# Reordering the start of a two-stage attention and MLP kernel: two weight blocks and the next batch's x change places in the load queue

## The chip, the cores and the metric

The kernel runs on one core of a Trainium2 chip. The metric is device time in microseconds (us) of one execution; less is better. A core has five engines that run side by side, each with its own in-order queue: TensorE (PE, matrix products, results to the small memory PSUM), VectorE (DVE), ScalarE (ACT), GpSimd (POOL) and SyncE (SP). They wait for each other by semaphores. Data moves between main memory and the on-chip SBUF by DMA.

## The reference

Two stages. In the first, for each of 8 batches and 8 heads, x (512 rows of 64) and a state (32 rows of 64) read each other; in the second, all 8 x 544 = 4352 rows of 512 go through a two-layer network with an exact gelu.

```python
scores = scale * x @ state.T          # scale = 1/8; softmax over 32
xread  = softmax(scores) @ state      # 512 x 64 per head
scores2 = scale * state @ x.T         # softmax over 512
sread  = softmax(scores2) @ x         # 32 x 64 per head
rows = concat([xread, sread], rows).to(4352, 512)
out  = gelu(rows @ w_in) @ w_out      # 512 -> 2048 -> 512
```

All inputs and the output are float32; the kernel computes in bfloat16 and sums in float32.

## The kernel before, in words

**The work.** The xread of a batch is never formed. Instead `pmat`/`p_mm` multiply the batch's state with `w_in` (a product P, in four column chunks f of 512; `p_copy` takes the two halves from PSUM to SBUF, one on ScalarE and one on VectorE), and `mm1(b, m)` multiplies P's block m of 128 columns with the transposed softmax weights AT and applies gelu on ScalarE to give block m (of 16) of g. `M(k)` is `mm1` of block k counted over all batches, so M(4) to M(7) are blocks 4 to 7 of batch 0 and M(16), M(17) blocks 0 and 1 of batch 1. The second layer of batch 0 is done by `mm2_m(0, m)`: block m of g times block m of `w_out`, four matmuls that add into four PSUM tiles. (From batch 1 on, the second layer is done by a scheme with seven products of quarter size, `X`, whose sums of weights `w_sums` and sums of g `g_sum` are made on VectorE.)

**The attention part of batch 1.** `begin(1)`; `xtr(1, ...)` transposes x on TensorE, 32 matmuls in two PSUM tiles, copied by VectorE to `xT`; `scores` multiplies it with the state and applies Exp on ScalarE to give `e`; `norm(1, half)` sums, inverts and scales `e` to `a` on VectorE; `atr(1)` transposes `a` into `AT`. `rearr_ones(1)` copies x into the layout `xo` that the state's reading needs, on VectorE for batches 0 and 1. `sread(b)` is that reading, 32 small matmuls of `e` with `xo` into the PSUM tile `sr`; `sread_out(b)` divides by the sums on VectorE to give `srm`; `srt(b)` transposes that and VectorE copies it to `XSR`, which the last batch's slot uses (`read_out_slot`, b = 7).

**The order.** It is written by hand: the calls from line 969 on are issued in the order they stand, and each engine runs its own instructions of them in that order. Nothing is rescheduled. Loads of weights, of x from batch 1 on and of the state (all but batch 0's) are issued from POOL's queue and land in the order of issue: first `w_in` columns 0 to 511, `w_out` blocks 0, 1, batch 1's state, blocks 2, 3, `w_in` 512 to 1023, then `load_x(1)`, and then `load_rest()`: blocks 4, 5, blocks 6, 7, `w_in` 1024 to 1535, blocks 8 to 11, `w_in` 1536 to 2047, batch 2's state, batch 2's x, blocks 12 to 15, batch 3's x. An issue waits for the landing of the one eight places before it, whose semaphore it takes over.

**PSUM.** There are eight banks. Four (`ps_f`, `ftile`) are a ring for short-lived tiles: `xT_ps`, `sr`, `pt`, `srT`, `p_ps`, `hp`, `aT_ps` of batch 1. The n-th tile waits until the (n-4)-th has been copied out. The other four (`ps_o`, `otile`) hold the four sums `op` of batch 0 until `mm2_m`/`U` end at group 15. `burst([...])` issues two products (four `ftile`s), then their four copies.

**ScalarE's tables.** Exp and Gelu need different tables; a switch is one ACT_TABLE_LOAD, 1.28 us. `exp_table()` forces a switch to Exp early by a one-element activation on `spare`.

**`warm`** is an SBUF tile of zeros for the dummy matmuls `keep_warm` before the first weights are there; it is not used after them.

The lines that the change moves stand at 126 to 143 (loads), 991 to 1067 (order), 1096 to 1114 and 1116 to 1132 (batch 2 and the loop over batches, eight slots p per batch). The functions follow.

Of the kernel before, what the change touches and what calls it, by code (L numbers as in the profile page):

```python
# [9 lines left out]
FP32 = mybir.dt.float32  # L10
BF16 = mybir.dt.bfloat16
AF = mybir.ActivationFunctionType
ALU = mybir.AluOpType
# [4 lines left out]
def kernel(  # L18
# [8 lines left out]
    nc = tc.nc  # L27
# [49 lines left out]
    sb0 = persist.tile([128, 2, 2, 2, NS], BF16, name="sb0")  # L77
    hold = persist.tile([128, 1], BF16, name="hold")
    spare = persist.tile([128, 1], FP32, name="spare")
    warm = persist.tile([128, 512], BF16, name="warm")  # L80
    xos = [persist.tile([128, SJ, HC, 132], BF16, name=f"xo_{i}") for i in range(2)]
    x4s = [persist.tile([128, SJ, HC, 128], BF16, name=f"x4_{i}") for i in range(2)]

# [28 lines left out]
    def load_w_out(m0, m1):  # L112
        nc.gpsimd.dma_start(out=w_out_bf[:, m0:m1, :], in_=w_out_r[:, m0:m1, :])  # L113

    def load_x(b):
        xb = xin.tile([128, H, SJ * D], BF16, name="xb", tag="xb")
        nc.gpsimd.dma_start(out=xb, in_=xr[b])
        xbs[b] = xb
# [13 lines left out]


    def load_rest():
        load_w_out(4, 6)
        load_w_out(6, 8)
        load_w_in(1024, 1536)
        load_w_out(8, 12)
        load_w_in(1536, 2048)
        load_st(2, 3)  # L140
        load_x(2)
        load_w_out(12, 16)
        load_x(3)
# [178 lines left out]
    def exp_table():  # L322
        nc.scalar.activation(out=spare, in_=spare, func=AF.Exp)
# [23 lines left out]
    def norm(b, half):  # L347
        A = atts[b]
        G = SJ * 2
        hs = slice(64 * half, 64 * half + 64)  # L350
        e4 = A.e[:, :, hs].rearrange("p g (c n) -> p g c n", n=NS)
        cs = att.tile([128, G, 2], FP32, name="cs", tag="cs")
        nc.vector.reduce_sum(out=cs, in_=e4, axis=AX.X)  # L353
        ics = att.tile([128, G, 2], FP32, name="ics", tag="ics")
        nc.vector.reciprocal(out=ics, in_=cs)
        nc.vector.tensor_tensor(  # L356
            out=A.a[:, :, hs].rearrange("p g (c n) -> p g c n", n=NS),
            in0=e4,
            in1=ics[:, :, :].to_broadcast((128, G, 2, NS)),
            op=ALU.mult,  # L360
        )
# [24 lines left out]
    def sread(b):  # L386
        A = atts[b]
        A.sr = ftile([128, 2, 65], "sr")
        for t in range(2):
            for j in range(SJ):  # L390
                for c in range(HC):
                    nc.tensor.matmul(  # L392
                        A.sr[32 * c:32 * c + 32, t, :],
                        lhsT=A.e[:, 2 * j + t, 32 * c:32 * c + 32],
                        rhs=A.xo[:, j, c, 1 + 65 * t:66 + 65 * t],
                        start=(j == 0),
                        stop=(j == SJ - 1),
                    )

    def sread_out(b):  # L400
        A = atts[b]
        A.srm = att.tile([128, 2, D], BF16, name="srm", tag="srm")
        flat = A.sr.rearrange("q t d -> q (t d)")
        inv = att.tile([128, 2], FP32, name="inv", tag="inv")
        nc.vector.reciprocal(out=inv, in_=flat[:, 0:130:129])
        nc.vector.tensor_tensor(
            out=A.srm,
            in0=flat[:, 1:129].rearrange("q (t d) -> q t d", t=2),
            in1=inv[:, :].to_broadcast((128, 2, D)),
            op=ALU.mult,  # L410
        )
# [31 lines left out]
    def pmat(b, f):  # L443
        p_copy(b, f, p_mm(b, f, ftile))
# [4 lines left out]
    def burst(chunks, b_read=None):  # L449
        done = []  # L450
        first = len(chunks) < 4 and b_read is not None
        if first:
            sread(b_read)
        for i, (b, f) in enumerate(chunks):
            done.append((b, f, p_mm(b, f, ftile if i < 2 else otile)))
        for x in done[:2]:
            p_copy(*x)
        if b_read is not None and not first:
            sread(b_read)
        for x in done[2:3]:  # L460
            p_copy(*x)
        if b_read is not None:
            sread_out(b_read)
        for x in done[3:]:
            p_copy(*x)
# [66 lines left out]
    def mm2_m(b, m):  # L532
        for j in range(SJ):
            if m == 0:
                ops[b, j] = otile([128, d_model], "op")
            nc.tensor.matmul(  # L536
                ops[b, j],
                lhsT=gs[b][:, m, j * 128:(j + 1) * 128],
                rhs=w_out_bf[:, m, :],
                start=(m == 0),  # L540
                stop=(m == MC - 1),
            )
# [16 lines left out]
    def w_sums(i):  # L559
        (b11, b12), (b21, b22) = w_q  # L560
        w_add(*(
            ("3", b12, b22, ALU.subtract),
            ("4", b21, b11, ALU.subtract),
            ("6", b11, b12, ALU.add),
            ("1", b11, b22, ALU.add),
            ("7", b21, b22, ALU.add),
        )[i])
# [347 lines left out]
    def M(*ms):  # L915
        for m in ms:
            mm1(m // MC, m % MC)
# [70 lines left out]
    keep_warm(6)  # L988
    sums0(1)
    norm0(0)  # L990
    load_x(1)
    scores0(3)
    sums0(2)
    sums0(3)
# [36 lines left out]
    burst([(1, 0), (0, 1)])  # L1031
    mm2_m(0, 3)
    M(4, 5)
    M(6)
    begin(1)
    xtr(1, (0, 1))
    xtr(1, (2, 3))
    sread(0)
    sread_out(0)
    M(7)  # L1040
    scores(1, 0)
    scores(1, 1)
    srt(0)
    mm2_m(0, 4)
    mm2_m(0, 5)
    rearr_ones(1)
    mm2_m(0, 6)
    norm(1, 0)
    sread(1)
    pmat(0, 2)  # L1050
    sread_out(1)
    norm(1, 1)
    mm2_m(0, 7)
    M(8, 9)
    M(10, 11)
    mm2_m(0, 8)
    atr(1)
    mm2_m(0, 9)
    w_sums(2)
    burst([(1, 1), (0, 3)])  # L1060
    mm2_m(0, 10)
    M(16, 17)
    M(12, 13)
    srt(1)
    M(14, 15)
    mm2_m(0, 11)
    w_sums(0)
# [30 lines left out]
    def home(shape, name):  # L1098
        at = next(homes)
        return ftile(shape, name) if at is None else otile(shape, name, at)  # L1100

    p0 = p_mm(2, 0, home)
    p1 = p_mm(2, 1, home)
    nc.scalar.copy(out=Ps[2][:, 1, 512:1024], in_=p1[1])
# [11 lines left out]
    for b in range(2, B):  # L1116
        nb = b + 1
        for p in range(8):
            k = 16 * b + 2 * p
            if p == 1 and nb < B:  # L1120
                scores(nb, 0)
                scores(nb, 1)
            if p in (2, 3) and nb < B:
                norm(nb, p - 2)
            if p == 3 and nb + 1 < B:
                xtr_dma(nb + 1)
            if p == 5 and nb < B:
                atr_dma(nb)
            if p == 7 and nb < B:
                srt(b)  # L1130
                if nb == B - 1:
                    srt(nb)
            if nb == B and p < 5:
                read_out_slot(p)
                if p == 4:
                    r_homes()
                    r_sum("5")
                    r_sum("2")
                continue
            M(k, k + 1)  # L1140
            if b == 2 and p in (0, 3):
                pmat(2, 2 + p // 3)
            if b == 2 and p == 1:
                w_sums(4)
            if p < 5:
                if p == 0:
                    g_sum(b - 1, "5")
                    if b > 2:
                        sr_w("5216"[b - 3])
                X(b - 1, "45127"[p])  # L1150
                if p < 3:
                    g_sum(b - 1, "127"[p])
            if p == 0 and b + 3 < B:
                hold_for(b, 0)
                load_x(4 if b == 2 else b + 3)
            if p == 6 and b == 2:
                hold_for(b, 12)
                load_x(5)
            if p == 0 and nb + 1 < B:
                begin(nb + 1)  # L1160
                rearr(nb + 1)
            if nb == B:
                if p == 5:
                    g_sum(b, "6")
                    R("3")
                    r_sum("1")
                    R("4")
                    r_sum("6")
                    r_sum("7")
                if p == 6:  # L1170
                    R("5")
                    X(b, "3")
                    R("2")
                    R("1")
                if p == 7:
                    R("6")
                    X(b, "6")
                continue
            if p == 5:
                g_sum(b, "6")  # L1180
                reads = (b, nb) if nb == B - 1 else (b,)
                for r in reads:
                    sread(r)
                p_run(nb, (0, 1), ((0, 1), (3, 2)))
                for r in reads:
                    sread_out(r)
                if b == 2:
                    rearr_ones(3)
                elif nb + 1 < B:
                    rearr_ones(nb + 1)  # L1190
            if p == 6:
                X(b, "3")
            if p == 7:
                if b == 2:
                    rearr_ones(4)
                p_run(nb, (2, 3), ((1, 2), None))
                X(b, "6")
# [41 lines left out]
```

## Time and profile before

| what | value |
|---|---|
| median of 3 runs | 203.81 us (203.44 to 204.97) |
| profiled execution, first to last instruction (its span) | 202.5 us |
| TensorE busy, share of the span | 196.6 us, 97% |
| VectorE / ScalarE / POOL busy | 157.1 (78%) / 135.4 (67%) / 67.9 us (34%) |
| TensorE clock granted | 1.00 throughout |
| DMA, 16.6 to 36 us | 187 to 207 GB/s |
| DMA, 52 to 202 us | 91 GB/s |

The profile gives for the profiled execution no other time than its span; the runs' times cover what lies around it as well. In its lines a row is one instruction or several merged ones: start in us from the span's beginning, duration in us (ns in group lists), the engine (PEld is TensorE's weight load), the line of the code, the operation, output tile <- input tiles, sizes, how many, and in brackets how long the engine stood idle before it and what ended that. A matmul's end is modelled, and matmuls overlap, so the distance between two starts tells the pace, not the duration.

### The profile page before, as it was taken

To read this page: it belongs to the slowest core of one execution; us is meant where nothing else is said; L and a number is where in the kernel's file an instruction comes from. 1 tells how busy PE (TensorE), PEld (TensorE's weight loads), DVE (VectorE), ACT (ScalarE), POOL (GpSimd) and SP (SyncE) were. 2 spreads that over 40 slices of the span, in tenths; PEclk is the share of its full clock that TensorE was granted. 3 is DMA by queue.
4 is the path that set the end of the run, shared out by engine and by line. 5 is a ranking of instruction groups with operands and counts; after the bars stand their busy time and mean duration, and the time that the engine had idled before them with its cause. 6 is when DMAs were issued, how large, how long until landed. Compare 5 with 4: busy or idle time off the path is not lost.

```text
span 202.5 us, 4900 instructions
## 1 busy us (share of the span) xinstructions
PE 196.6 (97%) x2035; PEld 132.6 (65%) x2035; DVE 157.1 (78%) x255; ACT 135.4 (67%) x240; POOL 67.9 (34%) x75
## 2 busy tenths in 40 slices
PE   7898999999999999999999999999999999999994
PEld 2433544465667577766776687567775787878893
DVE  2953776789998979878897787768778988895882
ACT  3785577699885779566967596687847576864120
POOL 8962603323249555360627502430220002200000
PEclk9999999999999999999999999999999999999999
DMA  6999999977675788782774308440107001040125
GB/s 203 174 174 203 205 199 197 181 134 142 96 135 107 207 104 108 155 179 32 90 163 142 77 0 123 130 119 0 52 9 202 3 0 55 0 159 0 52 102 162
DMA packets 40566, 23.16 MB, mean 114 GB/s; under 512 B 21856, under 2 KB 39136, under 8 KB 40544
## 3 DMA queue, kind: packets, MB, share of 16 engines
q0 software_dynamic: 13984, 8.10, 29.3%
q1 hardware_dynamic: 25872, 14.36, 28.5%
q10 hardware_dynamic: 688, 0.39, 0.6%
q8 instruction: 16, 0.26, 0.5%
q14 instruction: 6, 0.05, 0.1%
HBM read 17.30 MB, written 8.91 MB: 129 GB/s over the span
## 4 chain that ended last, share of the span: by engine, by line
PE 89%; DMA 5%; POOL 4%; DVE 0%; issue 0%; POOLq 0%
PE xp L591 41%; PE hp L494 26%; DMA xb<-in_x_dram 5%; PE p_ps L429 4%; PE op L536 4%; PE sp L798 3%; PE rp L864 3%; POOL w_in_bf L105 2%; PE op L520 2%; PE xp L703 2%; PE pt L333 2%; PE sr L392 1%; POOL sbd L95 1%; POOL w_out_bf L113 1%; PE xT_ps L271 1%; POOL st_bf L121 0%
## 5 line engine op out<-in xcount | busy, mean ns | idle before, releaser
L501 ACT ACTIVATE g<-hp 128x512 bf16<-128x512 f32 x124 | 67.1, 605 | 27.9 <-PE hp L494 21.3
L494 PE MATMUL hp<-AT,P 128*128 128x512 bf16 x248 | 62.9, 379 | 0.0
L591 PEld LDWEIGHTS <-gsum 128*128 128x128 bf16 x528 | 51.0, 98 | 12.1 <-issue 1.9
L585 DVE TENSOR_TENSOR gsum<-g 128x2048 bf16<-128x2048 bf16 x35 | 45.5, 1314 | 0.1
L591 PE MATMUL xp<-ws,gsum 128*128 128x256 bf16 x304 | 36.3, 273 | 0.0
L494 PEld LDWEIGHTS <-P 128*128 128x128 bf16 x248 | 22.8, 98 | 20.5 <-issue 2.7
L591 PE MATMUL xp<-ws,g 128*128 128x256 bf16 x224 | 26.8, 273 | 0.0
L591 PE MATMUL xp<-w_out_bf,gsum 128*128 128x256 bf16 x224 | 26.6, 273 | 0.0
L591 PEld LDWEIGHTS <-g 128*128 128x128 bf16 x224 | 21.7, 98 | 4.6 <-issue 0.2
L646 POOL TENSOR_TENSOR u<-s,oh 128x512 f32<-128x512 f32 x6 | 8.8, 1466 | 41.1 <-ACT oh L643 41.1
L441 DVE CAST P<-p_ps 128x512 bf16<-128x512 f32 x29 | 18.7, 683 | 3.1 <-PE p_ps L429 2.9
L440 ACT CAST P<-p_ps 128x512 bf16<-128x512 f32 x29 | 15.8, 599 | 5.4 <-PE p_ps L429 5.1
L225 POOL COPY x<-xb 128x1024 bf16<-128x1024 bf16 x12 | 12.6, 1080 | 15.7 <-DMA xb<-in_x_dram 15.7
L235 POOL COPY xo<-xb 128x1024 bf16<-128x1024 bf16 x12 | 14.5, 1234 | 4.6 <-PE sr L392 4.6
L610 POOL TENSOR_TENSOR v<-q,oh 128x512 f32<-128x512 f32 x6 | 8.6, 1434 | 20.6 <-ACT oh L648 20.5
L536 PE MATMUL op<-w_out_bf,g 128*128 128x512 bf16 x48 | 11.8, 380 | 0.0
L356 DVE TENSOR_TENSOR a<-e,ics 128x512 bf16<-128x512 bf16 x14 | 10.7, 764 | 0.5
L429 PE MATMUL p_ps<-w_in_bf,sbd 64*32 64x512 bf16 x248 | 10.5, 382 | 0.0
L353 DVE TENSOR_REDUCE cs<-e 128x16 f32<-128x512 bf16 x14 | 9.5, 677 | 0.7 <-ACT e L340 0.7
L419 DVE COPY XSR<-srT 128x128 bf16<-128x128 bf16 x8 | 5.7, 759 | 5.5 <-PE srT L416 5.5
L501 ACT ACT_TABLE_LOAD x7 | 9.0, 1283 | 0.1
L618 DVE TENSOR_TENSOR oh<-xp,v 128x512 f32<-128x512 f32 x6 | 4.1, 690 | 5.2 <-POOL v L610 5.2
(132 smaller groups left out, 230.2 us busy)
## 6 DMA issues: line engine op xcount, KB each, us to landing
out_dram<-oh SPq DMA_DIRECT2D x15, 256.0 KB, 2.9
xb<-in_x_dram POOLq DMA_DIRECT2D x7, 512.0 KB, 5.9
out_dram<-oh SPq DMA_DIRECT2D x6, 512.0 KB, 2.9
w_in_bf<-in_moe_w_in_dram POOLq DMA_DIRECT2D x6, 256.0 KB, 12.4
out_dram<-osb SPq DMA_DIRECT2D x5, 256.0 KB, 3.2
w_out_bf<-in_moe_w_out_dram POOLq DMA_DIRECT2D x4, 256.0 KB, 8.9
w_out_bf<-in_moe_w_out_dram POOLq DMA_DIRECT2D x2, 512.0 KB, 13.3
x0f<-in_x_dram SPq DMA_DIRECT2D x3, 256.0 KB, 3.7
```

The lines of the kernel that those rows point to most:

```text
L225: nc.gpsimd.tensor_copy(out=A.x4[:, :, :, 64 * t:64 * t + 64].rearrange("p j c d -> p c j d"), in_=src[:, t],)
L235: eng.tensor_copy(out=A.xo[:, :, :, 2 + 64 * t:66 + 64 * t].rearrange("p j c d -> p c j d"), in_=src[:, t],)
L353: nc.vector.reduce_sum(out=cs, in_=e4, axis=AX.X)
L356: nc.vector.tensor_tensor(out=A.a[:, :, hs].rearrange("p g (c n) -> p g c n", n=NS), in0=e4, in1=ics[:, :, :].to_broadcast((128, G, 2, NS) ...
L429: nc.tensor.matmul(ps[t][32 * c:32 * c + 32, :], lhsT=sbd[64 * t:64 * t + 64, b, c, 32 * t:32 * t + 32], rhs=w_in_bf[64 * t:64 * t + 64, c ...
L440: nc.scalar.copy(out=dst[:, 0, :], in_=ps[0])
L441: nc.vector.tensor_copy(out=dst[:, 1, :], in_=ps[1])
L494: nc.tensor.matmul(hp, lhsT=Ps[b][:, t, m * 128:(m + 1) * 128], rhs=atts[b].AT[:, :, t, :], start=(t == 0), stop=(t == 1),)
L501: nc.scalar.activation(out=gs[b][:, m, :], in_=hp, func=AF.Gelu)
L536: nc.tensor.matmul(ops[b, j], lhsT=gs[b][:, m, j * 128:(j + 1) * 128], rhs=w_out_bf[:, m, :], start=(m == 0), stop=(m == MC - 1),)
L585: nc.vector.tensor_tensor(out=t, in0=g_q(b, h0, k0), in1=g_q(b, h1, k1), op=op)
L591: nc.tensor.matmul(ps[:, j - js[0], :], lhsT=lhs[:, m, 128 * j:128 * j + 128], rhs=rhs[:, m, :], start=(first and j == js[0] and m == 0), ...
```

## The change

Batch 1's x and `w_out` blocks 4, 5 change places in POOL's queue. On TensorE, M(7) and the groups `mm2_m(0, 4)` and `mm2_m(0, 5)` are issued ahead of `xtr(1, ...)`, with an explicit `exp_table()` on ScalarE behind M(7)'s gelu. Groups 6 and 7 follow at the places where M(7) and groups 4, 5 stood, so that `pmat(0, 2)` is next to M(8). `norm(1, 1)` moves behind M(8) to M(11), M(16, 17) ahead of the burst, `w_sums(2)` behind the burst. The state reading of batch 1 moves: `sread(1)` down to the products of batch 2, with a ScalarE copy of its result into the memory of `warm`, and its division and transposing to slots 6 and 7 of batch 3.

```diff
     def load_rest():
-        load_w_out(4, 6)
+        load_x(1)
         load_w_out(6, 8)
...
+    def read_raw(b):
+        sread(b)
+        raw = persist.tile([128, 130], FP32, name="sraw", tag="warm")
+        nc.scalar.copy(out=raw, in_=atts[b].sr.rearrange("q t d -> q (t d)"))
+        return raw
+
+    def read_norm(b, raw):
+        A = atts[b]
+        A.srm = att.tile([128, 2, D], BF16, name="srm", tag="srm")
+        inv = att.tile([128, 2], FP32, name="inv", tag="inv")
+        nc.vector.reciprocal(out=inv, in_=raw[:, 0:130:129])
+        nc.vector.tensor_tensor(
+            out=A.srm,
+            in0=raw[:, 1:129].rearrange("q (t d) -> q t d", t=2),
+            in1=inv[:, :].to_broadcast((128, 2, D)),
+            op=ALU.mult,
+        )
...
     norm0(0)
-    load_x(1)
+    load_w_out(4, 6)
     scores0(3)
...
     M(4, 5)
-    M(6)
+    M(6, 7)
+    exp_table()
+    mm2_m(0, 4)
+    mm2_m(0, 5)
     begin(1)
     xtr(1, (0, 1))
     xtr(1, (2, 3))
     sread(0)
     sread_out(0)
-    M(7)
+    mm2_m(0, 6)
     scores(1, 0)
     scores(1, 1)
     srt(0)
-    mm2_m(0, 4)
-    mm2_m(0, 5)
+    mm2_m(0, 7)
     rearr_ones(1)
-    mm2_m(0, 6)
+    pmat(0, 2)
     norm(1, 0)
-    sread(1)
-    pmat(0, 2)
-    sread_out(1)
-    norm(1, 1)
-    mm2_m(0, 7)
     M(8, 9)
     M(10, 11)
+    norm(1, 1)
     mm2_m(0, 8)
     atr(1)
     mm2_m(0, 9)
+    M(16, 17)
+    burst([(1, 1), (0, 3)])
     w_sums(2)
-    burst([(1, 1), (0, 3)])
     mm2_m(0, 10)
-    M(16, 17)
     M(12, 13)
-    srt(1)
     M(14, 15)
...
+    raw1 = read_raw(1)
     p0 = p_mm(2, 0, home)
...
+            if b == 3 and p == 6:
+                read_norm(1, raw1)
             if p == 7 and nb < B:
                 srt(b)
+                if b == 3:
+                    srt(1)
```

More of the change, by code (lines that the diff above doesn't have):

```diff
@@ L79 @@
     spare = persist.tile([128, 1], FP32, name="spare")
-    warm = persist.tile([128, 512], BF16, name="warm")
+    warm = persist.tile([128, 512], BF16, name="warm", tag="warm")
     xos = [persist.tile([128, SJ, HC, 132], BF16, name=f"xo_{i}") for i in range(2)]
```

## The prediction

> **What bounds the kernel now.** I read three views in this order: the chain that ended last, to see which engine sets the end; TensorE's timeline from 17 to 31 us, where all the edits but two lie; and the timelines of ScalarE and VectorE over the same stretch, because an order on TensorE is only as good as the copies that feed it. First the chain's shares from the page, then its one long foreign piece from the chain in order of time:
>
> ```profile
> PE 89%; DMA 5%; POOL 4%; DVE 0%; issue 0%; POOLq 0%
> ```
>
> ```profile
> 8.93 10.95 DMA xb<-in_x_dram
> 19.87 0.04 issue
> 19.92 1.08 PE xT_ps L271 x32
> ```
>
> From 19.9 us on the chain is TensorE and nothing else, up to the last output's add. So every wait of TensorE after 17 us counts in full, work moved about on it counts nothing, and the only prize here is the idle time ahead of batch 1's transposes. TensorE's timeline gives its size (start, us, then in brackets the idle time before):
>
> ```profile
> 17.59 1.50 PE L494 MATMUL hp<-AT,P 128*128 128x512 bf16 x6
> 19.92 1.08 PE L271 MATMUL xT_ps<-ident,xb 128*64 128x128 bf16 x32 [0.82 <-DMA xb<-in_x_dram]
> 20.93 0.43 PE L392 MATMUL sr<-xo,e 128*32 128x65 bf16 x32
> 21.29 0.61 PE L494 MATMUL hp<-AT,P 128*128 128x512 bf16 x2
> 22.41 2.75 PE L536 MATMUL op<-w_out_bf,g 128*128 128x512 bf16 x12
> 25.46 0.41 PE L429 MATMUL p_ps<-w_in_bf,sbd 64*32 64x512 bf16 x8
> 25.80 1.04 PE L536 MATMUL op<-w_out_bf,g 128*128 128x512 bf16 x4
> 26.67 1.89 PE L494 MATMUL hp<-AT,P 128*128 128x512 bf16 x8
> 28.48 1.04 PE L536 MATMUL op<-w_out_bf,g 128*128 128x512 bf16 x4
> 29.35 0.61 PE L374 MATMUL aT_ps<-ident,a 128*128 128x128 bf16 x8
> ```
>
> Starts, not durations, give the pace: eight 512-column matmuls start 26.67 to 28.48, four `op` matmuls 25.80 to 26.67, so 0.216 us each; one lasts 0.38, so a group ends about 0.17 after its last start slot. Then ScalarE and VectorE:
>
> ```profile
> 18.27 1.57 ACT L501 ACTIVATE g<-hp 128x512 bf16<-128x512 f32 x3 [0.73 <-PE hp L494]
> 25.93 0.58 ACT L440 CAST P<-p_ps 128x512 bf16<-128x512 f32 x1 [1.00 <-PE p_ps L429]
> 26.53 1.28 ACT L501 ACT_TABLE_LOAD   x1
> 27.83 2.06 ACT L501 ACTIVATE g<-hp 128x512 bf16<-128x512 f32 x4
> ```
>
> ```profile
> 22.61 0.73 DVE L419 COPY XSR<-srT 128x128 bf16<-128x128 bf16 x1 [0.32 <-PE srT L416]
> 22.97 1.16 DVE L235 COPY xo<-xb 128x1024 bf16<-128x1024 bf16 x2
> 26.09 0.68 DVE L441 CAST P<-p_ps 128x512 bf16<-128x512 f32 x1
> 27.10 0.68 DVE L353 TENSOR_REDUCE cs<-e 128x16 f32<-128x512 bf16 x1
> 28.09 0.69 DVE L356 TENSOR_TENSOR a<-e,ics 128x512 bf16<-128x512 bf16 x1
> ```
>
> What to see: `pmat(0,2)` starts at 25.46 and M(8), which reads its copy, at 26.67, 1.21 later; `mm2_m(0,7)` fills that gap exactly. And `norm(1,1)` ends at 28.78, only 0.57 ahead of the transposes of `a` at 29.35. Both covers are thin, and the change takes both away.
>
> **The change part by part.** I follow TensorE through the new order with these durations.
>
> *The loads.* `w_out` blocks 4, 5 and batch 1's x swap places on POOL's queue. By the DMA view x was issued at 8.93 and landed at 19.87; blocks 4, 5 (9.81 plus 11.3) at 21.1; blocks 6, 7 at 22.4, each pair of blocks 1.3 after the one before; the last `w_in` piece ahead of them (8.32 plus 8.0) landed at 16.3. The queue lands in order, so blocks 4, 5 come at 16.3 + 1.3 = 17.6 and x takes their old place, 21.1. Everything behind them keeps its time. POOL's issue of x moves from 8.93 to about 9.6 behind one more 0.7 us issue, long before its data's turn. x took 3.5 us of the queue; the next batch's equal transfer took 2.7 (behind blocks of the same kind), so 20.3 to 21.7 bounds its landing. I take 21.1, the sum of the bytes ahead of it.
>
> *M(7) and groups 4, 5 ahead of the transposes.* M(4) to M(6) leave the issue slot at 19.92 - 0.82 - 0.17 = 18.93. M(7) adds 0.43, to 19.36; its `hp` buffer is the fourth `p_ps` of the burst, copied by 17.8. Groups 4 and 5 are 8 x 0.216 = 1.73, to 21.09; gelu 4 ended at 18.9 and gelu 5 at 19.4, so they don't wait. x at 21.1 plus an issue delay of 0.1: transposes at 21.2 in place of 19.92, 1.28 later with 0.44 + 1.73 = 2.17 us less left to do. **Gain 0.89**, 0.95 with x at 20.3, 0.35 with x at 21.7.
>
> *Reading 0, group 6, scores, group 7.* From 21.2: transposes 1.01 to 22.2, `sread(0)` 0.36 to 22.6 (blocks 6, 7 in by 22.4), group 6 0.87, scores 0.62, `srt(0)` 0.06, group 7 0.87 with 0.1 at a change of tile shape: `pmat(0,2)` starts at 25.05. Its `w_in` pieces land at 23.7 and 24.9. `exp_table()` puts the Exp load behind gelu 7, 20.3 to 21.7, ahead of the scores; the number of table loads is the same, and its dummy activation is 0.2 us of idle ScalarE. Nothing here costs TensorE.
>
> *`pmat(0,2)` straight before M(8).* The cover, group 7, now runs before it. M(8) still can't start until 1.21 after the first product matmul (the copy on ScalarE ends 1.05 after it), and the matmuls themselves take 0.34: **loss 0.87**, M(8) at 26.26. VectorE's half of the copy follows `rearr_ones` and lands at about the same time, so the bounds are 0.8 and 1.1. Behind M(8) the Gelu load (1.3 from start to start) puts gelu 8 at 27.42 to 28.03, group 8 at 28.1: 1.88 after M(8) where it was 1.81, **0.07**.
>
> The Trainium skill ("ScalarE: Activation LUTs", What ACT_TABLE_LOAD costs) puts a drain of about 1.38 us on top of the 1.28 us load for each switch of set. The rows above show the first gelu 1.30 after the load's start, so with no such drain; by the page, as an estimate, group 8 would start 1.4 later and the total would be 206.7.
>
> *`norm(1,1)` behind M(8) to M(11).* On VectorE the transposed reading of batch 0, `rearr_ones`, the copy of P, `norm(1,0)` and `norm(1,1)` are now one queue: 0.36 + 1.16 + 0.61 + 1.61 + 1.68 = 5.42 us by the starts above, from 24.3 (0.25 after `srt(0)` at 24.05). It ends at 29.7. TensorE is through with group 8 at 28.97 and `atr(1)` needs both halves: it starts at 29.75, **loss 0.75** (0.5 to 0.9). Taking `sread_out(1)` off this queue (0.4 us) is in the sum.
>
> *M(16, 17) ahead of the burst.* `ps_f` is a ring of four. After `atr(1)`'s two tiles come hp16, hp17, and the burst's four: the first product takes the two transposes' buffers, the second product those of hp16 and hp17, which stay full until gelu 16 and 17 are done. M(17) ends its slots at t = 0.86 after M(16)'s start; the first product would be issued by 1.2; gelu 16 runs from 0.62 to 1.22, gelu 17 from 1.11 to 1.71, and its release is seen at 1.78. Loss 1.78 - 1.18 = **0.60** (0.5 to 0.7). Before, the two tiles were long empty.
>
> *The later reading of batch 1.* `sread(1)` (0.36) and `srt(1)` (0.06) move down TensorE's queue and cost it the same. `read_raw`'s copy is one more ScalarE instruction of about 0.5 us ahead of a P copy near 48 us, where ScalarE runs without a gap from 41.8 to 50; TensorE has three groups queued there. Bounds 0 and 0.5; I take 0, since the copy it delays is read two groups later. `read_norm` is 0.45 us on VectorE, hidden by 22% idle. The second `srt` in the group at b = 3 makes two buffers of the ring wait for VectorE: where before has such a pair, at 155.5 us, the product behind it took 0.88 us in place of 0.56, so 0 to 0.32; I take 0.15.
>
> **Sum**: -0.89 + 0.87 + 0.07 + 0.75 + 0.60 + 0.15 = +1.55 us on a span of 202.5. The median of the runs shown, 203.81, is 1.3 above that span; what lies outside the span is not touched. 203.81 + 1.55 = 205.4, and as two of the losses were rounded up, I write 205.3. About 1% (2 us) is what a measurement of this kernel can tell from no change.
>
> **Rivals.**
> *Only the wait goes.* If the three covers hold after all, because copies end sooner than their rows or work slides into the gaps, the time is 203.81 - 0.89 = 202.9. For it: VectorE is 78% and ScalarE 67% busy. Against it: each of the three waits is one consumer straight behind its producer on the same in-order queue. Chance 0.12. It decides if the sum of the new waits is under 0.89; two of the three would have to be gone.
> *x comes late.* If x takes its place behind blocks 4, 5 and still needs more than its 3.5 us, or POOL's ring lets it in late, TensorE waits at the transposes in place of before, 0.1 for each 0.1 past 21.1, and all later waits stay: with x at 21.7 to 22.2, 205.9 to 206.4. Against it: the bytes ahead of x are known. It passes +1% from x at 21.6. Chance 0.23.
> *The edits don't act as described.* The built order shows the moved loads and groups where the diff puts them, so I give this nothing of its own.
>
> **Numbers.** The forecast, net +1.5 with own range 204.5 to 205.9, has 0.62; 0.03 is left for something faster still: in the windows by stage TensorE is busy for 2.50 of the 3.30 us from 16.6 to 19.9 and throughout from 19.9 to 52, so there is no 2 us to be had here. Range 202.9 to 206.5: the low end is the rival without losses, the high end x at 22.2. Faster by over 1%: 0.03. Slower by over 1%: most of the late-x case and the forecast's upper edge, 0.26. Within 1%: 0.71.
>
> **What would show it.** In the changed profile: transposes of x start at 21.0 to 21.3 with under 0.2 us idle before them; M(8) waits 0.8 to 1.0 on the P copy; `aT_ps` waits 0.5 to 0.9 on VectorE's `a`; `p_ps` of the burst waits about 0.6 on gelu; and TensorE has no other wait over 0.2 us up to 60 us. A transposes' start before 20.5, or no wait on M(8), would make the prediction wrong.

## The result and the profile after

| | median | runs | profiled execution: time, span |
|---|---|---|---|
| before | 203.62 us (203.31 to 204.97) | 6 | span 202.5 |
| changed | 206.03 us (205.55 to 206.60) | 6 | 206.49, span 204.7 |

The changed kernel takes 1.0108 times as long, with a 95% interval of 1.0083 to 1.0132: 2.2 us more. In the profiled executions with both a time and a span, the time is 1.77 us over the span (206.49 and 204.72 here, 203.54 and 201.77 in the second profile of before). So, as an estimate from these two, the execution that the prediction was worked out on, with its span of 202.49, took about 204.25 us, more than the median that the sum was then added to. That matters below.

TensorE's timeline of the changed kernel first (start, us, engine, line, operation, tiles, count, in brackets the idle time before it and what ended it):

```profile
17.86 1.89 PE L512 MATMUL hp<-AT,P 128*128 128x512 bf16 x8
19.59 1.89 PE L554 MATMUL op<-w_out_bf,g 128*128 128x512 bf16 x8
21.41 1.08 PE L271 MATMUL xT_ps<-ident,xb 128*64 128x128 bf16 x32
25.14 0.41 PE L447 MATMUL p_ps<-w_in_bf,sbd 64*32 64x512 bf16 x8
26.25 1.90 PE L512 MATMUL hp<-AT,P 128*128 128x512 bf16 x8 [0.70 <-ACT P L458]
28.16 1.04 PE L554 MATMUL op<-w_out_bf,g 128*128 128x512 bf16 x4
29.61 0.62 PE L374 MATMUL aT_ps<-ident,a 128*128 128x128 bf16 x8 [0.41 <-DVE a L356]
31.88 1.22 PE L447 MATMUL p_ps<-w_in_bf,sbd 64*32 64x512 bf16 x16
...
93.28 0.96 PE L447 MATMUL p_ps<-w_in_bf,sbd 64*32 64x512 bf16 x16
```

The wait for x is gone: groups 4 and 5 (19.59) run into the transposes (21.41). Two waits have brackets, 0.70 ahead of M(8) at 26.25 and 0.41 ahead of `aT_ps` at 29.61. Two more can only be read from a row's length, because the wait lies inside a merged row: sixteen product matmuls last 1.22 at 31.88 and 0.96 at 93.28, where the same sixteen take 0.62 or 0.63 when nothing holds them. The engines that TensorE waits for, ScalarE and VectorE:

```profile
25.61 0.59 ACT L458 CAST P<-p_ps 128x512 bf16<-128x512 f32 x1 [0.43 <-PE p_ps L447]
26.21 1.28 ACT L519 ACT_TABLE_LOAD   x1
27.51 2.06 ACT L519 ACTIVATE g<-hp 128x512 bf16<-128x512 f32 x4
31.56 1.09 ACT L519 ACTIVATE g<-hp 128x512 bf16<-128x512 f32 x2 [1.99 <-PE hp L512]
```

```profile
24.74 0.96 DVE L235 COPY xo<-xb 128x1024 bf16<-128x1024 bf16 x2
25.65 0.69 DVE L459 CAST P<-p_ps 128x512 bf16<-128x512 f32 x1
28.86 0.69 DVE L356 TENSOR_TENSOR a<-e,ics 128x512 bf16<-128x512 bf16 x1
```

ScalarE's half of P is done at 26.20 and M(8)'s first matmul, which reads it, follows at 26.25; VectorE's half is done at 26.34, ahead of the second matmul, which starts at 26.48. `a` ends at 29.55 and `aT_ps` follows at 29.61. Each is one consumer straight behind its producer. Inside the burst, the two tiles of the second product start at 32.21 and 32.70, each 0.05 after the end of a gelu, of block 16 (32.16) and of block 17 (32.65, the end of the last ScalarE row).

The kernel before was profiled a second time, in an execution of 203.54 us (span 201.8). It is the better yardstick, because in it x lands at 19.07 and not at 19.87:

```profile
19.12 1.08 PE L271 MATMUL xT_ps<-ident,xb 128*64 128x128 bf16 x32
25.87 1.89 PE L494 MATMUL hp<-AT,P 128*128 128x512 bf16 x8
28.55 0.61 PE L374 MATMUL aT_ps<-ident,a 128*128 128x128 bf16 x8
29.95 0.63 PE L429 MATMUL p_ps<-w_in_bf,sbd 64*32 64x512 bf16 x16
```

No bracket stands at 19.12: **in this execution of the kernel before there is no wait for x, the very thing that the change takes away.** (Its transposes start 0.05 after x lands, so x is only just in time.) From there on every start lies 0.80 to 0.82 earlier than in the first profile, to the end.

The end of the span moved too. SyncE's issues of the last outputs (start, us, queue, line, operation, tensors, count), from the timeline of the kernel before in its second profile, and then of the changed one:

```profile
197.30 1.86 SPq L662 DMA_DIRECT2D out_dram<-oh  x3
```

```profile
199.62 2.09 SPq L680 DMA_DIRECT2D out_dram<-oh  x3
```

The row of the same three issues, from the first's start to the last's end, is 2.09 long in place of 1.86, and in the DMA view of the last 6 us the last output of 64 KB on this queue needs 2.3 us from issue to landing in place of 1.9. From the start of the last add on VectorE to the last landing is 2.09 us in this profile of before and 2.74 in the changed kernel. Between these two profiles the last landing moved by 2.97 us: the last add comes 2.32 later, by TensorE, and the way out takes 0.65 longer.

### The profile page after: what moved, and what is told of

It is laid out like the page before. It is cut to its first block, busy times and chain, and to the rows that moved or that the text cites. A ratio compares the mean times of both kernels' runs of the same rounds, so it can differ in the third digit from the quotient of the medians.

```text
span 204.7 us, 4897 instructions
## 1 busy us (share of the span) xinstructions
PE 197.2 (96%) x2030; PEld 133.1 (65%) x2035; DVE 157.0 (77%) x255; ACT 135.8 (66%) x242; POOL 67.3 (33%) x75
## 4 chain that ended last, share of the span: by engine, by line
PE 90%; DVE 5%; DMA 2%; ACT 1%; issue 1%
PE xp L609 40%; PE hp L512 25%; PE p_ps L447 5%; PE op L554 4%; PE sp L816 3%; PE rp L882 3%; PE xp L721 2%; PE op L538 2%; DMA st_f<-in_state_dram 2%; PE pt L333 2%; PE sr L392 1%; PE hp L1027 1%; PE aT_ps L374 1%; DVE a L356 1%; DVE cs L353 1%
## 5 line engine op out<-in xcount | busy, mean ns | idle before, releaser
L512 PEld LDWEIGHTS <-P 128*128 128x128 bf16 x248 | 23.0, 98 | 21.2 <-issue 2.5
L609 PEld LDWEIGHTS <-g 128*128 128x128 bf16 x224 | 21.7, 98 | 4.6 <-issue 0.2
L447 PE MATMUL p_ps<-w_in_bf,sbd 64*32 64x512 bf16 x248 | 11.5, 383 | 0.1
L340 ACT ACTIVATE e<-pt 128x512 bf16<-128x512 f32 x14 | 7.6, 593 | 2.1 <-PE pt L333 2.0
```

The lines of the kernel that those rows point to most:

```text
L447: nc.tensor.matmul(ps[t][32 * c:32 * c + 32, :], lhsT=sbd[64 * t:64 * t + 64, b, c, 32 * t:32 * t + 32], rhs=w_in_bf[64 * t:64 * t + 64, c ...
L512: nc.tensor.matmul(hp, lhsT=Ps[b][:, t, m * 128:(m + 1) * 128], rhs=atts[b].AT[:, :, t, :], start=(t == 0), stop=(t == 1),)
L609: nc.tensor.matmul(ps[:, j - js[0], :], lhsT=lhs[:, m, 128 * j:128 * j + 128], rhs=rhs[:, m, :], start=(first and j == js[0] and m == 0), ...
```

## The experiments

Theory: the four new waits are additive and cost what their rows say, and the gain is the wait for x. Rivals: the waits are limited by something else than named (the layout copy `rearr_ones`, one P half), or the gain isn't there. Starts of chosen tiles in the profiled executions, in us; the last column is the time from the start of the last add to the last landing:

| kernel | x lands | transposes of x | M(8) | `aT_ps` | M(18) | M(48) | M(64) | last add | tail |
|---|---|---|---|---|---|---|---|---|---|
| before, first | 19.87 | 19.92 | 26.67 | 29.35 | 35.74 | 73.09 | 94.43 | 199.56 | 1.99 |
| before, second | 19.07 | 19.12 | 25.87 | 28.55 | 34.93 | 72.28 | 93.61 | 198.75 | 2.09 |
| changed | 20.21 | 21.41 | 26.25 | 29.61 | 36.50 | 74.20 | 95.93 | 201.07 | 2.74 |
| e1 | 20.17 | 21.21 | 26.05 | 29.40 | 36.30 | 74.00 | 95.72 | 200.85 | 2.65 |
| e2 | 21.46 | 21.50 | 26.34 | 29.70 | 36.00 | 73.72 | 95.44 | 200.58 | 2.71 |
| e3 | 20.81 | 21.23 | 26.08 | 29.43 | 36.33 | 74.03 | 95.36 | 200.55 | 2.72 |
| e4 | 21.93 | 21.97 | 27.20 | 30.49 | 37.38 | 75.08 | 96.81 | 201.95 | 2.93 |
| e5 | 20.02 | 20.07 | 26.82 | 29.50 | 35.88 | 73.23 | 94.56 | 199.70 | 1.99 |
| e6 | 19.90 | 20.93 | 26.45 | 29.59 | 35.97 | 73.31 | 94.65 | 199.78 | 2.00 |
| e7 | 20.64 | 20.79 | 25.77 | 29.02 | 35.32 | 73.03 | 94.37 | 199.55 | 1.99 |
| e9 | 19.14 | 19.18 | 25.93 | 28.62 | 35.00 | 72.34 | 93.68 | 198.82 | 2.13 |
| e10 | 19.66 | 21.28 | 25.71 | 30.88 | 34.78 | 72.48 | 93.82 | 199.01 | 2.73 |
| e11 | 19.84 | 21.26 | 26.95 | 30.71 | 37.66 | 75.00 | 96.34 | 201.48 | 2.39 |
| e12 | 19.79 | 19.83 | 26.23 | 29.13 | 35.42 | 73.12 | 94.85 | 199.99 | 2.93 |

Each ratio below is against runs of the kernel before on the same chip in the same sitting; their medians went from 203.69 to 204.36, so ratios are compared and not microseconds. (e1 to e4 ran on one chip, e5 to e8 on a second, e9 to e12 on a third; the second profile of before is e8.)

**One edit of the changed kernel undone at a time (e1 to e4).**

e1: the layout copy moved behind what was thought to wait for it.

```diff
-    rearr_ones(1)
     pmat(0, 2)
...
     atr(1)
+    rearr_ones(1)
```

> The changed kernel with rearr_ones(1) (two VectorE copies, 0.9 us) moved from ahead of the P copy to behind atr(1); only the state's reading at 47 us needs it now. Theory of the four waits: VectorE reaches norm(1,1) 0.9 us sooner, so the 0.41 us wait of the transposes of a goes; M(8) still waits for ScalarE's half of the P copy (ends 26.2), so that wait stays at 0.6 to 0.7; the kernel is 0.4 to 0.6 us faster than the changed one, 205.5. Rival, that the cost comes from the load order and not from VectorE: no change, 206.0. Rival, that VectorE's half of the P copy and not ScalarE's holds M(8): both waits go and it is 1.1 us faster, 204.9.

Measured: 206.34 us, ratio 1.0083 [1.0051, 1.0116]. The expectation for `aT_ps` failed:

```profile
29.40 0.62 PE L374 MATMUL aT_ps<-ident,a 128*128 128x128 bf16 x8 [0.41 <-DVE a L356]
```

The wait is the same 0.41. With the copy gone VectorE stands idle for 0.54 us ahead of its half of P, because P's product isn't there earlier; what leads up to `a` is product, P's copy (0.61 from start to start), `norm(1,0)` and `norm(1,1)` (1.6 each), all behind the product at 25. So the layout copy only filled time; `norm` is late because it stands behind the P copy. M(8)'s wait stayed at 0.70, by ScalarE's half.

e2: the burst ahead of M(16) and M(17) again.

```diff
-    M(16, 17)
     burst([(1, 1), (0, 3)])
     w_sums(2)
     mm2_m(0, 10)
+    M(16, 17)
```

> The changed kernel with M(16, 17) put back behind the burst and group 10. Theory: the two PSUM tiles of the second product are then those of hp10, hp11, long empty, so the 0.60 us inside the burst goes: 205.4. Rival, that the burst is long for another reason (its w_in piece lands late): no change, 206.0.

Measured: 205.98 us, 1.0059 [1.0033, 1.0085]. In the profile a hit: the burst is back at its full pace, and from `aT_ps` to M(18) it is 6.30 where the changed kernel takes 6.89.

```profile
31.12 0.63 PE L447 MATMUL p_ps<-w_in_bf,sbd 64*32 64x512 bf16 x16
```

e3: the two `srt` apart.

```diff
+            if b == 4 and p == 3:
+                srt(1)
...
-                if b == 3:
-                    srt(1)
```

> The changed kernel with srt(1) taken from beside srt(3) (batch 3, slot 7) to batch 4, slot 3. Theory: the product behind the pair no longer waits for VectorE's copies (0.96 us for its 16 matmuls back to 0.63), 0.33 us faster: 205.7. Rival, that a lone srt makes the same wait wherever it stands: no change, or the wait at its new place.

Measured: 205.69 us, 1.0063 [1.0023, 1.0103]. In the profile a hit: M(48) to M(64) takes 21.34 as before, not 21.73. By the ratios e2 and e3 are 1.0 and 0.9 us under the changed kernel where 0.60 and 0.33 were expected; intervals this wide do not size the two waits, the rows do.

e4: P's product ahead of group 7, the cover of before put back.

```diff
-    mm2_m(0, 7)
     rearr_ones(1)
     pmat(0, 2)
     norm(1, 0)
+    mm2_m(0, 7)
```

> The changed kernel with pmat(0,2) ahead of mm2_m(0,7), so that group 7 again lies between the product and M(8). If the lost cover alone were the cause, the 0.70 us wait goes: 205.3. By the queues it doesn't all go: the product's second tile waits for the scores' Exp (ends 24.7 where TensorE is there at 24.2), and VectorE's half of the P copy still stands behind rearr_ones and ends at 26.3: M(8)'s second matmul can't start before that, so 0 to 0.2 us faster: 205.9. The two differ by 0.6 us.

Measured: 206.08 us, 1.0088 [1.0054, 1.0122]. In the profiled execution, the slowest of the six at 207.62 us, the loads came late, so that TensorE waited for x (0.48), for `w_out` (0.32) and for `w_in`:

```profile
25.99 0.41 PE L447 MATMUL p_ps<-w_in_bf,sbd 64*32 64x512 bf16 x7 [0.40 <-DMA w_in_bf<-in_moe_w_in_dram]
```

M(8) doesn't wait here, but the product, now issued earlier, waits for its weights, and `aT_ps` still waits 0.37. The expected gain can't be read from this execution, and the interval, which overlaps the changed kernel's, shows none; it doesn't decide between the two expectations. The profile of e7, which has the same edit, does.

**The first half of the change, put into the kernel before (e5, e6).**

e5: only the loads change places.

```diff
     def load_rest():
-        load_w_out(4, 6)
+        load_x(1)
...
-    load_x(1)
+    load_w_out(4, 6)
```

> The kernel before with the two loads swapped and nothing else. x then lands at 20.2 to 21.1 in place of 19.9, TensorE is there at 19.1 to 19.2, so the transposes' wait grows from 0.82 to 1.1 to 2.0 and the kernel is 0.3 to 1.2 us slower than before; if the change's loss came from the load order (the late-x rival, or anything else that the order does to the queue), this kernel alone would show most of the 2.4 us.

Measured: 204.76 us, 1.0039 [1.0021, 1.0056]. x at 20.02, 0.95 after its landing in the second profile of before; TensorE waits 0.81 for it, less than the 1.1 to 2.0 expected. The 0.8 us in time are within the expected 0.3 to 1.2 and about a third of the changed kernel's loss. In the profile it is a wait for x, and the changed kernel's profile has none there, so by these profiles this isn't what the changed kernel loses.

e6: the loads, and M(7), groups 4 and 5 and `exp_table()` ahead of the transposes, nothing else (the loads as in e5).

```diff
-    M(6)
+    M(6, 7)
+    exp_table()
+    mm2_m(0, 4)
+    mm2_m(0, 5)
...
-    M(7)
...
-    mm2_m(0, 4)
-    mm2_m(0, 5)
```

> The kernel before with the loads swapped and M(7), groups 4, 5 and the early Exp table ahead of the transposes; the rest of the order is that of before, so group 6 stands behind rearr_ones and group 7 ahead of M(8). If only the wait for x goes: 0.9 us faster than before, 202.7. By the queues, the groups that hid VectorE's copies of xT behind the transposes are gone: the scores wait 0.3 to 0.7, srt(0) 0.2, the reading of batch 1 waits for xo 0.3 to 0.7, M(8) up to 0.6 for its copies: 1 to 1.5 us of new waits, so 0.1 to 0.6 us slower than before, about 204.

Measured: 205.07 us, 1.0059 [1.0039, 1.0079]; slower, not near 204. This kernel keeps the old order behind the transposes, and that order is now too short of work:

```profile
24.76 0.54 PE L392 MATMUL sr<-xo,e 128*32 128x65 bf16 x32 [0.31 <-DVE xo L235]
27.20 1.69 PE L494 MATMUL hp<-AT,P 128*128 128x512 bf16 x7 [0.38 <-DVE P L441]
```

Groups 4 and 5 had been the cover of the layout copy and of P's copy. Spent ahead of x, they are missing here: 0.31 and 0.38, and 0.19 at the scores.

**All losses undone at once (e7, e10).**

e7: the edits of e1, e2, e3 and e4 together.

```diff
-    mm2_m(0, 7)
-    rearr_ones(1)
     pmat(0, 2)
     norm(1, 0)
+    mm2_m(0, 7)
...
     atr(1)
+    rearr_ones(1)
     mm2_m(0, 9)
-    M(16, 17)
     burst([(1, 1), (0, 3)])
     w_sums(2)
     mm2_m(0, 10)
+    M(16, 17)
...
+            if b == 4 and p == 3:
+                srt(1)
...
-                if b == 3:
-                    srt(1)
```

> The changed kernel with the four late parts put right together: rearr_ones(1) behind atr(1), pmat(0,2) ahead of group 7, M(16, 17) behind the burst, srt(1) apart from srt(3). Theory: of the four waits (0.70, 0.5, 0.60, 0.33) all but about 0.5 at the product's second tile go, so 1.6 us faster than the changed kernel, 204.4; if the gain at x's wait is 0.9 as summed, it stands 0.3 us under before, 203.3. The two statements can't both hold unless 0.8 to 1.1 us of the changed kernel's loss is still there: that would be what the four waits don't explain.

Measured: 204.29 us, 1.0035 [1.0013, 1.0057]. By the ratios 1.5 us under the changed kernel, near what was expected, but 0.7 above before, not under it. Two waits are left in its profile:

```profile
24.56 0.41 PE L447 MATMUL p_ps<-w_in_bf,sbd 64*32 64x512 bf16 x7 [0.52 <-ACT e L340]
29.02 0.62 PE L374 MATMUL aT_ps<-ident,a 128*128 128x128 bf16 x8 [0.41 <-DVE a L356]
```

The first is the one expected of e4 as well: ahead of group 7 the product meets the Exp of the scores. The second stayed, as in e1, though the expectation counted it as gone. Together they are 0.93, and the last add is 0.80 later than in the second profile of before: with the other losses gone, no gain of 0.89 shows.

e10: the best order that the rows suggested: group 7 split in halves around the product (`mm2_m` takes the sums to be done as a third argument), groups 9, 10 and the burst used as cover for `norm`, M(16, 17) and `rearr_ones` behind that, `srt(1)` apart as in e3.

```diff
-    mm2_m(0, 7)
-    rearr_ones(1)
+    mm2_m(0, 7, (0, 1))
     pmat(0, 2)
+    mm2_m(0, 7, (2, 3))
...
     mm2_m(0, 8)
+    mm2_m(0, 9)
+    burst([(1, 1), (0, 3)])
+    mm2_m(0, 10)
     atr(1)
-    mm2_m(0, 9)
+    M(12, 13)
+    rearr_ones(1)
+    w_sums(2)
     M(16, 17)
-    burst([(1, 1), (0, 3)])
-    w_sums(2)
-    mm2_m(0, 10)
-    M(12, 13)
     M(14, 15)
```

> The changed kernel put right once more, with what the runs showed: group 7 in two halves around pmat(0,2), atr(1) behind groups 9, 10 and the burst, M(16, 17) behind M(12, 13), rearr_ones(1) behind those, srt(1) apart. By the queues the transposes of a and the burst wait no more, M(8) 0.4 us: 1.5 us under the changed kernel in TensorE's time, 204.3 with the late end as it is, 203.7 without. Against the kernel before (203.7, whose wait for x is near 0 in its usual run) that is 0 to 0.7 us slower. If the gain at x's wait were the summed 0.89 in the usual run, it would be 0.5 us faster than before.

Measured: 204.33 us, 1.0015 [0.9996, 1.0035]. M(8) is the only long row with a foreign releaser left up to 50 us:

```profile
25.71 1.90 PE L512 MATMUL hp<-AT,P 128*128 128x512 bf16 x8 [0.16 <-ACT P L458]
```

Even so the last add is 0.26 later than in the second profile of before: an order with practically no waits isn't faster than an execution of before with x at 19.1, which has none either. Against executions in which before does wait it may be. In this profile the way out takes 2.73, 0.64 longer than in that of before; whether every execution of e10 pays that isn't shown, and if most do, TensorE's part is some tenths shorter than in the median execution of before.

**The late end (e8, e9), and the reading (e11, e12).** The trace's DMA packets show a possible reason for the slower way out: a queue of kind "instruction" brings 16 KB pieces, and the last of them runs into the last outputs. It starts 1.9 to 2.1 us before the last add and takes 0.93 us in the two profiles of before; in the changed kernel it starts 2.6 before and takes 1.85.

e8 is the kernel before, unchanged, profiled again.

> The kernel before, unchanged, for a second profile: its last output lands about 1.7 us after it is issued, as in the first profile, if the 2.4 us of the changed kernel have a real part of 0.75 us at the very end; if the end scatters from run to run, it differs here by some tenths.

Measured: 203.54 us in its one run, x at 19.07, end and fetch as in the first profile. This run shows the wait for x to be a matter of the single execution.

e9 adds two one-element copies on ScalarE to the kernel before, to shift the count of its instructions.

```diff
+    for _ in range(2):
+        nc.scalar.copy(out=spare, in_=spare)
```

> The kernel before with two copies of one element added on ScalarE, in the 1.8 us at 14.7 us in which it is idle; they do nothing. In the profiles of the changed kernel and of three of its variants the last 16 KB instruction fetch starts 2.6 us ahead of the last output's add and takes 1.8 us, in those of the kernel before 2.0 us ahead and 0.9 us; the last output then lands 2.7 us after that add in place of 2.0. The changed kernel has two instructions more on ScalarE. Theory that this count shifts the fetch into the last outputs: TensorE's times stay, the fetch moves to 2.6 ahead, and the kernel is 0 to 0.7 us slower, 203.7 to 204.4. Rival, that the end depends on something else in the changed kernel: fetch and end as before, 203.7.

Measured: 204.11 us, 0.9995 [0.9971, 1.0018]. The fetch stays at 1.88 before the last add and the end at 2.13. The count of ScalarE's instructions isn't it. Its profiled execution (203.63 us) is also a third look at the old load order: x at 19.14, no wait.

e11 puts only the reading of batch 1's state back into the changed kernel.

```diff
     rearr_ones(1)
+    sread(1)
     pmat(0, 2)
     norm(1, 0)
+    sread_out(1)
...
     M(12, 13)
+    srt(1)
     M(14, 15)
...
-    raw1 = read_raw(1)
...
-            if b == 3 and p == 6:
-                read_norm(1, raw1)
...
-                if b == 3:
-                    srt(1)
```

> The changed kernel with only the reading of batch 1's state put back: sread(1) between rearr_ones(1) and pmat(0,2), sread_out(1) behind norm(1,0), srt(1) between M(12,13) and M(14,15). Both theories: the wait at b=3 goes (M(64) starts 21.3 after M(48), as before, instead of 21.7: -0.33), the wait for aT of batch 1 grows by what sread_out puts on VectorE ahead of norm(1,1), about +0.4, so TensorE ends about where it ended in the changed kernel, within 0.2. Theory 1, the late reading moves TensorE's last instruction fetch into the output's end: that fetch starts about 2.0 before the last add, the last transfer lands 2.0 to 2.1 after it, and the time is about 205.4. Theory 2, the late end comes from elsewhere in the order: fetch 2.6 before the last add, landing 2.65 or more after it, time 205.9 to 206.2.

Measured: 206.86 us, 1.0137 [1.0103, 1.0171]. The double `srt` is gone (M(48) to M(64) 21.34). In its place:

```profile
25.37 0.54 PE L392 MATMUL sr<-xo,e 128*32 128x65 bf16 x32 [0.31 <-DVE xo L235]
26.95 1.47 PE L512 MATMUL hp<-AT,P 128*128 128x512 bf16 x6 [0.70 <-ACT P L458]
29.11 0.59 PE L512 MATMUL hp<-AT,P 128*128 128x512 bf16 x2 [0.68 <-DVE srm L406]
30.71 0.62 PE L374 MATMUL aT_ps<-ident,a 128*128 128x128 bf16 x8 [0.15 <-DVE a L356]
```

Neither theory had the third line: `sr` is a tile of the ring of four, it stays full until `sread_out(1)` has read it behind `norm(1,0)`, and M(11) needs its place, 0.68 later. (The rule given ahead, that a tile waits for the fourth one before it, doesn't hold to the letter: `sr` stands six tiles before that of M(11).) 0.31 + 0.68 + 0.15 = 1.14, against 0.41 + 0.33 in the changed kernel: 0.40 more, and the last add is 0.41 later. The late reading thus earns its cost in the new order, by these rows; the intervals of the two kernels overlap. The fetch starts 2.61 before the last add and the end takes 2.39: the early fetch is there without the late reading.

e12 puts only the late reading into the kernel before.

```diff
-    sread(1)
...
-    sread_out(1)
...
-    srt(1)
...
+    raw1 = read_raw(1)
...
+            if b == 3 and p == 6:
+                read_norm(1, raw1)
...
+                if b == 3:
+                    srt(1)
```

> The kernel before with only the late reading of batch 1's state: its copy read_raw ahead of the P copy, read_norm at b=3, srt(1) straight beside srt(3). Both theories: the wait of 0.33 at the double srt appears (M(64) 21.7 after M(48)), sread_out leaves VectorE's row ahead of norm(1,1), and TensorE has no other new wait; +0.1 to +0.35 on TensorE. Theory 1, the late reading alone makes the late end: the last fetch starts about 2.6 before the last add and the last transfer lands 2.65 or more after it; about 0.9 over the kernel before (ratio 1.0045). Theory 2: fetch at 2.0 and landing at 2.0 to 2.1, 0.1 to 0.35 over the kernel before (ratio 1.0005 to 1.0017).

Measured: 204.57 us, 1.0014 [0.9990, 1.0038]. The wait at b = 3 came as expected:

```profile
92.20 0.96 PE L447 MATMUL p_ps<-w_in_bf,sbd 64*32 64x512 bf16 x16
```

The fetch starts 2.61 before the last add, takes 2.03 and the end takes 2.93, as theory 1 had it for the profiled execution; but the median is 0.3 over before, as theory 2 had it. So the late end of the one profiled execution is not shown to be paid by the others. In the profiles, then, the late reading alone brings the early fetch, and so does the new order without it (e11): theory 1 in its strict form falls. Over all profiles the end follows the fetch. In the five of before, e5, e6 and e9, which start it 1.85 to 2.06 before the last add, it takes 0.93 to 0.96 and the end 1.99 to 2.13. In the nine others, which start it 2.59 to 2.69 before:

```
              e7    e11   e3    e10   e2    e1    changed  e12   e4
fetch takes   1.19  1.50  1.77  1.80  1.82  1.83  1.85     2.03  2.03
end takes     1.99  2.39  2.72  2.73  2.71  2.65  2.74     2.93  2.93
```

That is a correlation; no run moves the fetch alone, and what moves its start stays open.

## Why the prediction was right or wrong, by its own steps

The time of 206.03 lies 0.7 above the predicted 205.3 and inside the stated range, but just outside the forecast's own 204.5 to 205.9; the range reached so far for a late x, which the profile doesn't show, so that the time fell inside it is in part luck. The costs came by the forecast's mechanism, covers too thin for the new order; the small gain at x did not come. In its own frame, the first profile of before, TensorE's sum was +1.55 and M(64), behind all the covers, came 1.50 later. What was wrong lies in one term of the sum, in what the sum was added to, and behind TensorE's end. Of the signs that it named, the wait of the burst was as told; the transposes' start (21.41 for 21.0 to 21.3), M(8)'s wait (0.70 for 0.8 to 1.0) and, by its bracket, that of `aT_ps` (0.41 for 0.5 to 0.9) each missed their interval by about 0.1.

- **The loads.** x was put at 21.1 with 20.3 to 21.7 as bounds; it landed at 20.21 in the profile of the changed kernel, just under them, and between 19.66 and 21.93 in the nine other profiles with this order of loads. In the changed kernel's, the last `w_in` piece ahead landed at 16.61, blocks 4, 5 at 17.51, 0.90 later where the sum had 1.3, and x 2.70 after them where it had 3.5. The transposes were told for 21.2 and started at 21.41: it was groups 4 and 5 that they waited for, from an M(4) 0.27 later, not x.
- **The gain of 0.89: the step that failed.** It is the wait of 0.82 in one execution, in which x landed at 19.87. In two further profiles of the old load order, with x at 19.07 and 19.14, the transposes start at 19.12 and 19.18 with no wait. Against 19.12 the changed kernel's 21.41 is 2.29 later with 2.17 less left to do: no gain at all. The old order does show such a wait in some executions (e12: 0.55 with x at 19.79), so it is worth 0 to 0.8 by execution. And the sum was made on the profiled execution, with the wait in it, but added to the median of 203.81, which stands only 0.27 above the execution without a wait (203.54) and 0.44 under the estimate for this one (204.25); added to that it would have been 205.8. The bound of 0.35 for x at 21.7 should by the same sum be 0.29.
- **`pmat` straight before M(8), +0.87.** The wait is there, 0.70 by its bracket and 0.77 by starts, on the copy that was named; M(8) was told for 26.26 and came at 26.25, with the two errors ahead of it cancelling. Group 8 behind the Gelu load, +0.07: 28.16 is 1.91 after M(8), +0.10. With the product ahead of group 7 this wait goes (e4, e7), but the product then waits 0.52 itself (e7); half of group 7 as cover leaves 0.16 (e10).
- **`norm(1,1)`, +0.75.** By starts 0.58, by the bracket 0.41, inside 0.5 to 0.9 by the first. The queue was named rightly, but the layout copy in its sum was not what counted (e1): a sum along an in-order queue must begin at the last input that was late, here the product.
- **M(16), M(17) ahead of the burst, +0.60.** 1.22 in place of 0.62, with the two tiles released by gelu 16 and 17 as told, and 0.59 back when undone (e2). Right.
- **The reading.** The double `srt`, +0.15 of bounds 0 to 0.32: 0.33, and 0.39 back with e3, which also moves the 0.06 of the `srt` itself. The row at 155.5 us was the right one, and the upper bound the right value. The copy on ScalarE cost nothing that shows. That the later reading also spares the ring a wait of 0.68 in the new order (e11) was not seen.
- **No other wait over 0.2 us up to 60 us:** held.
- **The end, costed at nothing:** +0.65 in the profiled execution. This was not in the sum at all. The text put what lies outside the span as untouched; it was inside the span, after the last add.

The costs measured 0.70 + 0.10 + 0.58 + 0.60 + 0.33 = 2.31 against 2.44 told. With no gain they make the 2.32 by which TensorE ends later than in the second profile of before. The table has this step by step, against that profile: M(8) is 0.38 later (its wait, with the 0.36 of `sread(1)` gone from ahead of it), `aT_ps` 1.06, M(18) 1.57 (with `srt(1)` gone), M(48) 1.92 (the reading is back), M(64) 2.32 (so is `srt(1)`). The end's 0.65 makes it 2.97; the medians differ by 2.41, as the profiled execution of the changed kernel, 206.49, is 0.46 above its median and this one of before, 203.54, 0.08 below. So the medians' difference, 2.2 by the ratio, is no more than TensorE's part alone, and whether the end's part is in it stays open.

Of the rivals, "Only the wait goes" is excluded by the brackets. "x comes late" gave a time that fits, 205.9 to 206.4, but not its mechanism: there is no wait for x in the profile. It is seen in single executions (0.20 in e2, 0.48 in e4).

The page "ScalarE: Activation LUTs" of the Trainium skill (What ACT_TABLE_LOAD costs) would have added a drain of about 1.38 us to the load. The changed kernel's rows again don't show it: the load starts at 26.21 and the first gelu at 27.51, 1.30 later.

## What to carry to other kernels

A wait for a transfer that one profile shows may be that execution's own: where a change rests on it alone, profile the kernel twice, and make the sum against the time of the very execution that the terms come from. Work moved forward to fill a wait is taken from where it was a cover; before moving it, list for each producer and consumer around it what stands between them afterwards, and count the places of the ring of tiles as consumers too. Where the sum of an in-order queue is made, begin at the input that comes last, not at the first instruction of the row.

## What the runs showed that was not expected

- The landing of the same x on the same queue varied between executions from 19.07 to 19.87 with the old order of loads, and from 19.66 to 21.93 with the new one; the three latest, 20.81 to 21.93, are of the one chip of e1 to e4, and with one profile a kernel the chip's part and the execution's can't be told apart. In the two profiles of before x lands 3.54 and 3.46 after the `w_in` piece ahead of it (16.33 and 15.61), so nearly all of the 0.80 between them arose ahead of x. TensorE has no slack behind it, so 0.8 us of the 1.7 by which the runs of the kernel before differ (203.31 to 204.97) can come from this alone.
- The last 16 KB piece of instructions takes 0.93 us or up to 2.03, and the last output lands 2.0 or up to 2.9 us after the last add's start, the two together. The Trainium skill says ("Runtime: NRT & Kernel Launch", Instruction fetch mechanics) that the crossing of such a block is mostly hidden. TensorE shows no wait for it here either; what goes with it is the time that the output's transfers take.
